# A gated delta rule feeding routed experts: the chunk recurrence as a hand-ordered pipeline of stages

## The chip, the cores and the metric

The kernel runs on one core of a Trainium2 chip. The metric is the device time of one execution in microseconds (us). Before the change the median of three runs is 1243.71 us (1240.04 to 1244.63).

## What is computed

All data is float32: `q`, `k`, `v` of (4, 8, 768, 48) (batch, heads, positions, head size) and `beta` of (4, 8, 768). A delta rule runs over the positions of each head, with a 48x48 state:

```
k_n = k / (norm(k) + 1e-06)
for t in range(S):
    y[t]  = q[t] @ state
    v_old = state.T @ k_n[t]
    state = state + beta[t] * outer(k_n[t], v[t] - v_old)
```

The eight heads of a position are then one row `x` of 384 values (3072 rows). A router takes the best of 8 experts by cosine, with the softmax weight of the best; each expert is `relu(x @ w1[e]) @ w2[e]` with 1024 hidden units, weighted by the router's weight.

## The kernel before, in words

**Attention.** Positions are taken in 12 chunks of 64 (`C`). A tile's 128 partitions hold the 64 positions of one chunk of two batches (g = 0, 1), so that two tiles (p = 0, 1) cover the four batches; the free dimension holds 8 heads by 48. Two chunks make a superchunk (6 of them), and a superchunk's four tiles are numbered j.

`front(s)` (L197) does what needs no state: it loads K, Q, V (`load`, L185), squares and sums the keys (L206, L207), takes the root with GpSimd's pow (L208), scales the keys (L217) and multiplies them by beta (L220), transposes keys and queries on TensorE (L231), multiplies K by K and Q (L239), and masks both products with beta (L245 for A, L246 for P).

`invert(s, A)` (L252) needs the inverse of (1 + A) for each chunk and head. Its four 32x32 diagonal blocks per pair of chunks go through DRAM (`a_dram`, L257, L260), so that 128 partitions hold 128 blocks; VectorE eliminates row by row in 31 steps of two instructions (L267, L269); the inverses go back through DRAM (`t_dram`, L271, L273), are transposed (L275), and TensorE builds the lower 32x32 blocks from them (L285 to L295).

`step(s, j, ...)` (L299) is the recurrence of one tile: the state times keys and queries (L319), the residual R (L321), the solve Z (L329), the new state (L341, added on VectorE in L343), the outputs (L348, L351), then their squares, transposes and router products (L353 to L363). `route(s, ...)` (L365) works out expert, weight and slot of the four tiles, writes the rows to `x_dram` (L395), and scatters the row numbers into `idmap` with four indirect DMAs (L415).

**Order.** Each engine takes its instructions in one fixed order and waits for whatever the head of its queue needs. The tile framework's scheduler orders them by priority around the program's text, which asks for `front` and `invert` of the next superchunk ahead of the four steps of this one:

```
        if s + 1 < NS:
            ahead = front(s + 1)
            Wn = invert(s + 1, ahead[0])
        for j in range(J):
            step(s, j, kts[j], pts[j], kbs[j], vs[j], W, xc, ssx, lz)
        route(s, xc, ssx, lz)
```

**Experts.** Afterwards the rows are processed in 19 tiles of 256 slots: `fetch` (L473) reads the slots of a tile from `idmap`, gathers its rows (L485) and loads its expert's weights (L479, L481); `experts` (L489) transposes (L496), multiplies (L503, L509) and scatters the results (L513). The change does not touch this stage.

Of the kernel before, what the change touches and what calls it, by code (L numbers as in the profile page):

```python
# [15 lines left out]
C = 64  # L16
# [5 lines left out]
def kernel(  # L22
# [28 lines left out]

    nc = tc.nc
# [7 lines left out]
    NS, J = NC // 2, 2 * P2  # L60

    cpool = ctx.enter_context(tc.tile_pool(name="const", bufs=1))
    ps = ctx.enter_context(tc.tile_pool(name="ps", bufs=1, space=bass.MemoryType.PSUM))
    x_dram = tc.dram_tile([N + 1, Dm + 1], F32, name="x_dram")
    idmap = tc.dram_tile([NMAP, 1], I32, name="idmap")
    a_dram = tc.dram_tile([2, 4, J * H, Q, Q], F32, name="a_dram")
    t_dram = tc.dram_tile([2, 4, J * H, Q, Q], F32, name="t_dram")

    def two():
        return ps.tile([128, 2, 512], F32, name="two", tag="two", bufs=3)  # L70

    def one(shape):
        return ps.tile(shape, F32, name="one", tag="one", bufs=2)
# [6 lines left out]
    half = cpool.tile([128, J, H], F32, name="half")  # L80
# [30 lines left out]
    ac = att.enter_context(tc.tile_pool(name="ac", bufs=1))  # L111

    with tc.tile_pool(name="pre", bufs=1) as pre:
        bt = pre.tile([P2 * H, NC, 2, C], F32, name="bt")
        for p in range(P2):
            for g in range(2):
                nc.scalar.dma_start(out=bt[p * H:(p + 1) * H, :, g, :],
                                    in_=beta[2 * p + g].rearrange("h (c t) -> h c t", t=C))
        emb = pre.tile([E, Dm], F32, name="emb")
        nc.scalar.dma_start(out=emb, in_=moe_expert_emb)  # L120
        rtau = ac.tile([128, 1], F32, name="rtau")
        nc.scalar.dma_start(out=rtau, in_=moe_tau.broadcast_to([128, 1]))
        nc.vector.reciprocal(rtau, rtau)

        psB = one([128, NC, P2 * H])
        for c in range(NC):
            nc.tensor.transpose(psB[:, c, :], bt[:, c].rearrange("p g t -> p (g t)"), ident[0:P2 * H, 0:P2 * H])
        betaT = ac.tile([128, NC, P2, H], F32, name="betaT")
        nc.vector.tensor_copy(betaT.rearrange("p c b h -> p c (b h)"), psB)


        esq = pre.tile([E, Dm], F32, name="esq")
        ess = pre.tile([E, 1], F32, name="ess")
        nc.scalar.activation(esq, emb, ACT.Square, accum_out=ess)
        nc.gpsimd.tensor_tensor(out=ess, in0=ess, in1=half[0:E, 0, 0:1], op=ALU.pow)
        nc.vector.tensor_scalar_add(ess, ess, 1e-6)
        nc.vector.reciprocal(ess, ess)
        nc.vector.tensor_scalar_mul(esq, emb, ess)
        psE = one([128, KC, E])
        for j in range(KC):  # L140
            nc.tensor.transpose(psE[:, j, :], esq[:, j * 128:(j + 1) * 128], ident[0:E, 0:E])
        enT = ac.tile([128, KC, E], F32, name="enT")
        nc.vector.tensor_copy(enT, psE)

    io = att.enter_context(tc.tile_pool(name="io", bufs=2))
    wk = att.enter_context(tc.tile_pool(name="wk", bufs=2))
# [4 lines left out]
    nc.vector.tensor_scalar(later[0:C, 0, :], mask_su[0:C, 0:C], 1.0, None, op0=ALU.mult)  # L151
# [8 lines left out]
    eye = ac.tile([128, Q, Q], F32, name="eye")  # L160
    nc.gpsimd.memset(eye, 0.0)
    nc.gpsimd.affine_select(out=eye, in_=eye, compare_op=ALU.not_equal, fill=1.0, base=0,
                            pattern=[[1, Q], [-1, Q]], channel_multiplier=0)


    Qs, KNs, KBs, PIs = [], [], [], []
    for i in range(4):
        Qs.append(ac.tile([128, H, 64], F32, name=f"Qp{i}"))
        nc.gpsimd.memset(Qs[i], 0.0)
    for i in range(4):  # L170
        KNs.append(ac.tile([128, H, 64], F32, name=f"KN{i}"))
# [12 lines left out]

    def load(c):  # L185
        Ks, Vs = [], []
        for p in range(P2):
            Kt = io.tile([128, H, D], F32, name="K", tag="K", bufs=4)
            Vt = io.tile([128, H, D], F32, name="V", tag="V", bufs=8)
            for dst, src in ((Kt, k), (Qs[(c * P2 + p) % len(Qs)][:, :, 0:D], q), (Vt, v)):  # L190
                for g in range(2):
                    nc.sync.dma_start(out=dst[64 * g:64 * g + 64],
                                      in_=src[2 * p + g, :, c * C:(c + 1) * C, :].rearrange("h t d -> t h d"))
            Ks.append(Kt)
            Vs.append(Vt)
        return Ks, Vs


    def front(s):

        data = [load(2 * s + i) for i in range(2)]
        rn = wk.tile([128, J, H], F32, name="rn", tag="rn")
        for j in range(J):
            Ksq = wk.tile([128, H, D], F32, name="Ksq", tag="Ksq")
            Kt = data[j // P2][0][j % P2]
            nc.gpsimd.tensor_tensor(Ksq, Kt, Kt, op=ALU.mult)  # L206
            nc.vector.tensor_reduce(rn[:, j], Ksq, axis=AX.X, op=ALU.add)  # L207
        nc.gpsimd.tensor_tensor(out=rn, in0=rn, in1=half, op=ALU.pow)  # L208
        nc.vector.tensor_scalar_add(rn, rn, 1e-6)
        nc.vector.reciprocal(rn, rn)  # L210
        A = wk.tile([128, J, H, C], F32, name="A", tag="A")
        kts, pts, kbs, vs = [], [], [], []
        for j in range(J):
            c, p = 2 * s + j // P2, j % P2
            n = c * P2 + p
            kn, kb, qp = KNs[n % len(KNs)], KBs[n % len(KBs)], Qs[n % len(Qs)]
            nc.gpsimd.tensor_tensor(kn[:, :, 0:D], data[j // P2][0][p],  # L217
                                    rn[:, j].unsqueeze(2).broadcast_to([128, H, D]), op=ALU.mult)
            bh = betaT[:, c, p]
            nc.gpsimd.tensor_tensor(kb[:, :, 0:D], kn[:, :, 0:D], bh.unsqueeze(2).broadcast_to([128, H, D]),  # L220
                                    op=ALU.mult)
            mb = wk.tile([128, 2, NP, C], F32, name="mb", tag="mb")
            for hh in range(2):
                nc.gpsimd.tensor_tensor(mb[:, hh], later.broadcast_to([128, NP, C]),
                                        bh.rearrange("p (a b) -> p b a", b=2)[:, hh].unsqueeze(2)
                                        .broadcast_to([128, NP, C]), op=ALU.mult)
            KQ = wk.tile([128, NP, 2, 2, C], F32, name="KQ", tag="KQ", bufs=8)
            for i, src in enumerate((kn, qp)):
                psT = one([128, NP, 2, C])
                for hp in range(NP):  # L230
                    nc.tensor.transpose(psT[:, hp].rearrange("p g t -> p (g t)"),  # L231
                                        src[:, 2 * hp:2 * hp + 2, :].rearrange("p h d -> p (h d)"), ident)
                nc.scalar.activation(KQ[:, :, :, i, :], psT, ACT.Copy)
            psG = two()
            for hp in range(NP):
                for g in range(2):
                    for hh in range(2):
                        r = slice(64 * hh, 64 * hh + D)
                        nc.tensor.matmul(psG[64 * g:64 * g + 64, hh, 128 * hp:128 * hp + 128],  # L239
                                         lhsT=KQ[r, hp, g, 0, :], rhs=KQ[r, hp, g, :, :],  # L240
                                         start=True, stop=True, skip_group_check=True)
            pg = psG.rearrange("p a (b i t) -> p (a b) i t", i=2, t=C)
            Pt = wk.tile([128, H, C], F32, name="P", tag="P", bufs=8)
            mbf = mb.rearrange("p a b t -> p (a b) t")
            nc.vector.tensor_tensor(A[:, j], pg[:, :, 0, :], mbf, op=ALU.mult)  # L245
# [307 lines left out]
```

## Time and profile before

| | us |
|---|---|
| median of the runs | 1243.71 |
| the profiled execution | 1250.58 |
| its span, first to last instruction | 1248.6 |
| TensorE busy in the span | 781.4 |
| VectorE busy | 304.9 |
| ScalarE busy | 160.7 |
| GpSimd busy | 240.6 |

The profiled execution lies 0.55% above the median, and 2 us of it lie outside the span. PE is TensorE's matmuls, PEld its weight loads, DVE is VectorE, ACT ScalarE, POOL GpSimd, SP the sync engine that issues most DMAs. The clock is the share of TensorE's full clock that was granted: 1.00 is 2.4 GHz, 0.50 is 1.2 GHz.

### The profile page before, as it was taken

To read this page: it belongs to the slowest core of one execution; us is meant where nothing else is said; L and a number is where in the kernel's file an instruction comes from. 1 tells how busy PE (TensorE), PEld (TensorE's weight loads), DVE (VectorE), ACT (ScalarE), POOL (GpSimd) and SP (SyncE) were. 2 spreads that over 40 slices of the span, in tenths; PEclk is the share of its full clock that TensorE was granted. 3 is DMA by queue.
4 is the path that set the end of the run, shared out by engine and by line. 5 is a ranking of instruction groups with operands and counts; after the bars stand their busy time and mean duration, and the time that the engine had idled before them with its cause. 6 is when DMAs were issued, how large, how long until landed. Compare 5 with 4: busy or idle time off the path is not lost. (4 is left out here: it accounts for less than half of the span.)

```text
span 1248.6 us, 18748 instructions
## 1 busy us (share of the span) xinstructions
PE 781.4 (63%) x8033; PEld 632.4 (51%) x8033; DVE 304.9 (24%) x821; ACT 160.7 (13%) x313; POOL 240.6 (19%) x259
## 2 busy tenths in 40 slices
PE   0306128801980088209813985299999999999996
PEld 0206028601870077208703885276766766767764
DVE  3471440344033502360243022001001001011010
ACT  0102012200220022002201221010100100101100
POOL 5553400231013201300110011111111111111110
PEclk9755555655555555655565555599999999999998
DMA  4522310331025101410111010654554455455520
GB/s 83 110 42 44 72 34 8 56 68 34 8 48 83 34 8 35 71 34 9 39 34 35 2 27 26 215 179 154 175 187 156 159 180 179 138 175 181 167 70 0
DMA packets 167668, 104.93 MB, mean 84 GB/s; under 512 B 133089, under 2 KB 155801, under 8 KB 167586
## 3 DMA queue, kind: packets, MB, share of 16 engines
q1 hardware_dynamic: 161232, 91.28, 27.2%
q0 software_dynamic: 5632, 12.24, 3.5%
q8 instruction: 63, 1.03, 0.4%
q10 hardware_dynamic: 722, 0.23, 0.1%
q14 instruction: 19, 0.16, 0.1%
HBM read 87.84 MB, written 18.63 MB: 85 GB/s over the span
## 5 line engine op out<-in xcount | busy, mean ns | idle before, releaser
L285 PE MATMUL one<-Tz,A 64*64 64x32 f32 x768 | 45.7, 291 | 313.5 <-ACT Tz L277 313.5
L503 PE MATMUL two<-xTm,w 128*128 128x256 f32 x912 | 203.4, 383 | 12.3 <-DVE xTm L497 12.3
L285 PEld LDWEIGHTS one<-Tz,A 64*64 64x64 f32 x768 | 43.7, 222 | 314.6 <-ACT Tz L277 314.6
L509 PE MATMUL one<-w,hT 128*128 128x384 f32 x608 | 199.2, 486 | 0.0
L503 PEld LDWEIGHTS two<-xTm,w 128*128 128x128 f32 x912 | 172.8, 191 | 40.0 <-DVE xTm L497 17.0
L509 PEld LDWEIGHTS one<-w,hT 128*128 128x128 f32 x608 | 115.5, 190 | 76.5
L512 DVE TENSOR_SCALAR y<-one,xg 128x384 f32<-128x384 f32 x38 | 23.5, 618 | 389.5 <-PE one L509 389.5
L505 ACT ACTIVATE hT<-two 128x512 f32<-128x512 f32 x76 | 45.4, 597 | 412.6 <-PE two L503 412.6
L513 POOL DMA_INDIRECT out_dram<-y,ids x38 | 38.1, 1004 | 242.4 <-DVE y L512 242.4
L267 DVE TENSOR_TENSOR tmp<-Bk,Tk 128x31 f32<-128x31 f32 (+15 forms) x186 | 71.1, 382 | 52.5 <-DMA Bk<-a_dram 46.6
L269 DVE TENSOR_TENSOR Tk<-Tk,tmp 128x31 f32<-128x31 f32 (+15 forms) x186 | 68.2, 367 | 5.9
L485 POOL DMA_INDIRECT xg<-x_dram,ids x38 | 37.3, 982 | 133.1 <-DMA ids<-idmap 84.7
L319 PE MATMUL two<-S,KQ 48*64 48x48 f32 x1408 | 56.8, 294 | 6.5 <-DVE P L246 6.5
L220 POOL TENSOR_TENSOR KB<-KN,betaT 128x384 f32<-128x384 f32 x24 | 20.5, 859 | 206.0 <-PE two L341 206.0
L293 PE MATMUL one<-Wd,PI 64*64 64x32 f32 x768 | 46.1, 292 | 14.6 <-ACT PI L288 14.6
L319 PEld LDWEIGHTS two<-S,KQ 48*64 48x64 f32 x1408 | 47.6, 202 | 13.2 <-issue 12.2
L343 DVE TENSOR_TENSOR S<-S,two 128x384 f32<-128x384 f32 x22 | 12.2, 554 | 168.7 <-PE two L341 168.7
L293 PEld LDWEIGHTS one<-Wd,PI 64*64 64x64 f32 x768 | 42.8, 220 | 17.8 <-ACT PI L288 17.8
L329 PE MATMUL one<-R,W 64*64 64x48 f32 x768 | 49.2, 303 | 0.0
L277 ACT ACTIVATE Tz<-Td,first 128x1024 f32<-128x1024 f32 x6 | 6.9, 1148 | 324.8 <-DMA Td<-t_dram 324.8
L329 PEld LDWEIGHTS one<-R,W 64*64 64x64 f32 x768 | 47.0, 223 | 0.1
L348 PE MATMUL two<-Z,P 64*64 64x48 f32 x768 | 46.3, 303 | 0.7 <-ACT Z L332 0.6
(129 smaller groups left out, 758.2 us busy)
## 6 DMA issues: line engine op xcount, KB each, us to landing
w<-in_moe_w_dram SPq DMA_DIRECT2D x38, 1536.0 KB, 6.7
x_dram<-xc SPq DMA_DIRECT2D x24, 192.5 KB, 3.1
Qp<-in_q_dram SPq DMA_DIRECT2D x48, 96.0 KB, 4.2
K<-in_k_dram SPq DMA_DIRECT2D x48, 96.0 KB, 2.7
V<-in_v_dram SPq DMA_DIRECT2D x48, 96.0 KB, 2.7
a_dram<-A SPq DMA_DIRECT2D x24, 128.0 KB, 2.8
Bk<-a_dram SPq DMA_DIRECT2D x6, 512.0 KB, 3.7
t_dram<-Tk SPq DMA_DIRECT2D x6, 512.0 KB, 2.6
```

Of the source, the lines that this page charges most:

```text
L267: nc.vector.tensor_tensor(tv, Bk[:, i, i + 1:Q].unsqueeze(2).broadcast_to(sh), Tk[:, i:i + 1, 0:i + 1].broadcast_to(sh), op=ALU.mult)
L269: nc.vector.tensor_tensor(Tk[:, i + 1:Q, 0:i + 1], Tk[:, i + 1:Q, 0:i + 1], tv, op=ALU.subtract)
L285: nc.tensor.matmul(psP[r, h, :], lhsT=A[r, j, h, :], rhs=Tz[r, j * H + h, :], start=True, stop=True, skip_group_check=True)
L293: nc.tensor.matmul(psW[r, h, :], lhsT=PI[r, h, :], rhs=Wd[r, j * H + h, :], start=True, stop=True, skip_group_check=True)
L319: nc.tensor.matmul(pv[64 * g:64 * g + 64, hh, hp, :], lhsT=KQ[r, hp, g, i, :], rhs=Sp[r, g, hp, :], start=(hp == 0), stop=True, skip_group ...
L329: nc.tensor.matmul(psZ[r, h, :], lhsT=W[r, j * H + h, :], rhs=Rf[r, h, :], start=True, stop=True, skip_group_check=True)
L348: nc.tensor.matmul(yv[r, hh, hp, :], lhsT=Pt[r, hh * NP + hp, :], rhs=Z[r, hh * NP + hp, :], start=(c == 0 and hp == 0), stop=True, skip_g ...
L485: nc.gpsimd.indirect_dma_start(out=x, out_offset=None, in_=x_dram[:, :], in_offset=bass.IndirectOffsetOnAxis(ap=ids[:, t:t + 1], axis=0))
L503: nc.tensor.matmul(psH[:, 0, i * T:(i + 1) * T], lhsT=w1[:, j, (f + i) * 128:(f + i + 1) * 128], rhs=xT[:, j, :], start=(j == 0), stop=(j ...
L505: nc.scalar.activation(hT[:, f:f + 2, :], psH[:, 0].rearrange("p (i t) -> p i t", i=2), ACT.Relu)
L509: nc.tensor.matmul(psO, lhsT=hT[:, f, t * 128:(t + 1) * 128], rhs=w2[:, f, :], start=(f == 0), stop=(f == NF - 1))
L513: nc.gpsimd.indirect_dma_start(out=out[:, :], out_offset=bass.IndirectOffsetOnAxis(ap=ids[:, t:t + 1], axis=0), in_=y, in_offset=None, bou ...
```

## The change

The attention part is written anew, as stages per chunk c, inside a region in which each engine takes its instructions in the order of the text. One iteration of the loop issues the norms of chunk c+6, the transposes and products of c+5, part of an elimination, the lower blocks of c+1, and the recurrence of c; it runs from c = -6 to 11. The elimination is a generator, of which `steps(n)` issues n steps. Routing takes four chunks at once (8 tiles) and is a generator too, worked off by `fill(n)`; it ends with eight indirect DMAs. Beta leaves keys and masks: `weigh` multiplies the blocks by it and starts the inverse from it. The state of two heads is block-diagonal, so that one product of 128 rows by 96 columns takes the place of two of 48 by 48. The sum of the states stays in PSUM, and ScalarE copies it to SBUF (`keep`). Keys are loaded twice (`Kf` and `Kl`), and Q in halves.

```diff
+    def squares(c):
...
+            nc.gpsimd.tensor_tensor(Ksq, Kf[c][p], Kf[c][p], op=ALU.mult)
...
+            nc.vector.tensor_reduce(rns[c][:, p], sq[p], axis=AX.X, op=ALU.add)
...
+    def root(c):
+        nc.gpsimd.tensor_tensor(out=rns[c].rearrange("p a h -> p (a h)"), in0=rns[c].rearrange("p a h -> p (a h)"),
+                                in1=half, op=ALU.pow)
...
+    def blocks_in(s):
+        Bks[s] = wk.tile([128, Q, Q], F32, name="Bk", tag="Bk")
+        nc.sync.dma_start(out=Bks[s], in_=a_dram[s % 2].rearrange("b i n s t -> (b i n) s t"))
+
+    def weigh(s):
+        Tks[s] = wk.tile([128, Q, Q], F32, name="Tk", tag="Tk")
+        nc.gpsimd.memset(Tks[s], 0.0)
+        nc.gpsimd.tensor_copy(Tks[s].rearrange("p a b -> p (a b)")[:, 0:Q * Q:Q + 1], bb[:, s])
+        nc.gpsimd.tensor_tensor(Bks[s], Bks[s], bb[:, s].unsqueeze(1).broadcast_to([128, Q, Q]), op=ALU.mult)
...
+    def by_state(ps1, c, p, i):
+
+        for hp in range(NP):
+            for g in range(2):
+                nc.tensor.matmul(ps1[64 * g:64 * g + 64, 2 * D * hp:2 * D * (hp + 1)], lhsT=KQs[c, p][:, hp, g, i, :],
+                                 rhs=state(c, p)[:, g, hp].rearrange("p a d -> p (a d)"),
+                                 start=(hp == 0), stop=True, skip_group_check=True)
...
+    def keep(c, p):
+        for hh in range(2):
+            r = slice(64 * hh, 64 * hh + D)
+            nc.scalar.activation(state(c + 1, p)[r, :, :, hh, :], sv[r, :, p], ACT.Copy)
...
+        yield
         for j in range(J):
             nc.gpsimd.indirect_dma_start(
                 out=idmap[:, :], out_offset=bass.IndirectOffsetOnAxis(ap=slot_i[:, j:j + 1], axis=0),
...
+    for c in range(-6, NC):
+        cf, cn, cl = c + 5, c + 6, c + 1
+        odd = c % 2 == 1
+        if odd and 0 <= (c + 1) // 2 < NS:
+            inverses_back((c + 1) // 2)
+        if odd:
+            elim = eliminate((c + 3) // 2) if 0 <= (c + 3) // 2 < NS else None
+        if has(cn):
+            squares(cn)
+        if has(cl):
+            if c < 0:
+                Kl[cl], Vl[cl] = load(k, cl, "Kl", 2), load(v, cl, "V", 4)
+            unit_keys_again(cl, 0)
+        if has(cn):
+            root(cn)
+        if has(cl):
+            unit_keys_again(cl, 1)
+        if has(c):
+            Rs = [residual(c, p) for p in both]
+        if has(cf):
+            transposes(cf, 0, 0)
+            transposes(cf, 0, 1)
+            transposes(cf, 1, 0)
+        steps(3)
+        if has(c):
+            solve(c, 0, Rs[0])
+        if has(cf):
+            transposes(cf, 1, 1)
+        if has(c):
+            solve(c, 1, Rs[1])
+        if has(cf):
+            products(cf, 0)
+        steps(3)
+        if has(cn):
+            inverse_norms(cn)
+            unit_keys(cn)
+            load_q(cn) if cn > 0 else None
+        if has(cn + 2):
+            Kf[cn + 2] = load(k, cn + 2, "K", 4)
+        if has(c + 2) and c + 1 >= 0:
+            Kl[c + 2], Vl[c + 2] = load(k, c + 2, "Kl", 2), load(v, c + 2, "V", 4)
+        if has(c) and c < NC - 1:
+            for p in both:
+                update(c, p)
+        if has(cf):
+            products(cf, 1)
+            blocks_out(cf)
+            if cf % 2 == 1:
+                blocks_in(cf // 2)
+                weigh(cf // 2)
+        if has(c) and c < NC - 1:
+            for p in both:
+                keep(c, p)
+        steps(3)
+        if odd and 0 <= (c + 1) // 2 < NS:
+            turn((c + 1) // 2)
+        fill(6)
+        if has(c):
+            outputs(c, 0)
+            steps(3)
+            fill(6)
+            outputs(c, 1)
+        steps(20 if not odd else 4)
+        if has(cl):
+            lower1(cl)
+        if has(c):
+            store(c)
+            xTs = [turned(c, p) for p in both]
+        if has(cl):
+            lower2(cl)
+        if has(c):
+            for p in both:
+                squared(c, p)
+            logits(c, xTs)
+            fill(20)
+            if c % RC == RC - 1:
+                behind.append(route(c // RC))
+    fill(1000)
```

## Rows read from the trace of the kernel before

**Rows 1.** Busy time by stretch: length, busy us of each engine, clock, DMA share, GB/s.

```profile
306.00:434.00 128.00, 61.46 (x1096) 55.70 (x1096) 42.06 (x115) 18.90 (x39) 26.32 (x27) 0.54 0.21 38
...
802.00:1249.00 447.00, 416.33 (x1634) 301.63 (x1632) 43.00 (x76) 45.38 (x76) 73.52 (x74) 0.98 0.47 155
```

**Rows 2.** The same view, inside the period of 306 to 434 us.

```profile
306.00:325.00 19.00, 14.96 (x264) 14.43 (x266) 1.25 (x1) 5.54 (x10) 0.00 (x0) 0.50 0.01 2
325.00:362.00 37.00, 33.50 (x608) 30.58 (x606) 4.73 (x12) 8.56 (x21) 4.35 (x5) 0.50 0.09 18
362.00:380.00 18.00, 12.88 (x229) 10.69 (x229) 9.14 (x31) 4.79 (x9) 5.74 (x7) 0.78 0.49 90
380.00:434.00 54.00, 0.11 (x8) 0.00 (x0) 26.94 (x71) 0.00 (x0) 16.23 (x15) 0.50 0.28 48
```

**Rows 3.** Who waited for whom: total us, times, longest.

```profile
PE one L285 <- ACT Tz L277: 313.5, 6, 58.4
```

**Rows 4.** The timeline of that period's inverse: start us, us, engine, line.

```profile
385.97 2.24 SPq L257 DMA_DIRECT2D a_dram<-A  x4
397.83 0.19 DVE L267 TENSOR_TENSOR tmp<-Bk,Tk 128x31 f32<-128x31 f32 x1 [10.84 <-DMA Bk<-a_dram]
...
430.08 0.19 DVE L269 TENSOR_TENSOR Tk<-Tk,tmp 128x31 f32<-128x31 f32 x1
437.31 1.15 ACT L277 ACTIVATE Tz<-Td,first 128x1024 f32<-128x1024 f32 x1 [61.44 <-DMA Td<-t_dram]
```

**Rows 5.** Groups of instructions: busy us, mean ns, idle before.

```profile
L267 DVE TENSOR_TENSOR tmp<-Bk,Tk 128x31 f32<-128x31 f32 (+15 forms) x186 | 71.1, 382 | 52.5 <-DMA Bk<-a_dram 46.6
L269 DVE TENSOR_TENSOR Tk<-Tk,tmp 128x31 f32<-128x31 f32 (+15 forms) x186 | 68.2, 367 | 5.9
L343 DVE TENSOR_TENSOR S<-S,two 128x384 f32<-128x384 f32 x22 | 12.2, 554 | 168.7 <-PE two L341 168.7
L206 POOL TENSOR_TENSOR Ksq<-K 128x384 f32<-128x384 f32 x24 | 20.5, 855 | 60.5 <-DMA K<-in_k_dram 44.6 <-DVE rn L207 15.7
L208 POOL TENSOR_TENSOR rn<-rn,half 128x32 f32<-128x32 f32 x6 | 33.0, 5504 | 23.4 <-DVE rn L207 23.4
```

**Rows 6.** Timeline, the first superchunk's inverse comes back.

```profile
99.57 1.15 ACT L277 ACTIVATE Tz<-Td,first 128x1024 f32<-128x1024 f32 x1 [54.30 <-DMA Td<-t_dram]
```

**Rows 7.** Timeline: an elimination step beside GpSimd, and the same form alone.

```profile
72.44 1.96 POOL L220 TENSOR_TENSOR KB<-KN,betaT 128x384 f32<-128x384 f32 x2
72.78 0.93 DVE L267 TENSOR_TENSOR tmp<-Bk,Tk 128x252 f32<-128x252 f32 x1
...
80.51 0.42 DVE L267 TENSOR_TENSOR tmp<-Bk,Tk 128x252 f32<-128x252 f32 x1
```

**Rows 8.** Timeline: eight K loads in a row on the SP queue.

```profile
394.19 5.36 SPq L192 DMA_DIRECT2D K<-in_k_dram  x8
```

**Rows 9.** Stretches around the rise of the clock, columns as in rows 1.

```profile
117.80:120.60 2.80, 2.80 (x15) 2.28 (x12) 0.00 (x0) 1.58 (x3) 0.83 (x1) 0.50 0.00 0
120.60:129.00 8.40, 7.18 (x150) 5.58 (x148) 4.42 (x7) 3.37 (x6) 6.41 (x10) 1.00 0.54 100
```

**Rows 10.** Timeline: TensorE at either clock, transposes (L231) and products (L239).

```profile
117.84 1.11 PE L231 MATMUL one<-ident,KN 128*128 128x128 f32 x4
...
367.92 1.99 PE L239 MATMUL two<-KQ 48*64 48x128 f32 x32
371.17 1.10 PE L239 MATMUL two<-KQ 48*64 48x128 f32 x32 [0.25 <-ACT KQ L233]
```

**Rows 11.** Timeline, from the last attention output to the first expert tile.

```profile
764.89 0.50 ACT L351 ACTIVATE xc<-two 128x384 f32<-128x384 f32 x1 [2.04 <-PE two L348]
774.52 1.03 POOL L415 DMA_INDIRECT idmap<-tokid,slot_i  x1 [7.35 <-DVE ends L455]
...
791.72 0.38 SPq L477 DMA_DIRECT2D ids<-idmap  x1
801.64 1.51 PE L496 MATMUL one<-ident,xg 128*128 128x128 f32 x6 [30.25 <-DMA xg<-x_dram,ids]
```

More of the change, by code (lines that the diff above doesn't have):

```diff
@@ L79 @@
     nc.vector.memset(ones, 1.0)
-    half = cpool.tile([128, J, H], F32, name="half")
+    half = cpool.tile([128, P2 * H], F32, name="half")
     nc.vector.memset(half, 0.5)
@@ L111, with bank @@
     ac = att.enter_context(tc.tile_pool(name="ac", bufs=1))
-    with tc.tile_pool(name="pre", bufs=1) as pre:
-        bt = pre.tile([P2 * H, NC, 2, C], F32, name="bt")
+    wk = att.enter_context(tc.tile_pool(name="wk", bufs=2))
+    ps = att.enter_context(tc.tile_pool(name="ps", bufs=1, space=bass.MemoryType.PSUM))
+    def bank(tag, bufs):
+        return ps.tile([128, 512], F32, name=tag, tag=tag, bufs=bufs)
+    Qs, KNs = [], []
+    for i in range(P2):
+        Qs.append(ac.tile([128, NP, 2, 64], F32, name=f"Qp{i}"))
+        nc.gpsimd.memset(Qs[i], 0.0)
+        KNs.append(ac.tile([128, NP, 2, 64], F32, name=f"KN{i}"))
+        nc.gpsimd.memset(KNs[i], 0.0)
@@ L115, with heads, load, load_q @@
+    def heads(t):
+        return t.rearrange("p (a b) d -> p b a d", a=2)
+    def load(src, c, name, bufs):
+        ts = []
+        for p in range(P2):
+            t = wk.tile([128, H, D], F32, name=name, tag=name, bufs=bufs)
+            for g in range(2):
+                nc.sync.dma_start(out=t[64 * g:64 * g + 64],
+                                  in_=src[2 * p + g, :, c * C:(c + 1) * C, :].rearrange("h t d -> t h d"))
+            ts.append(t)
+        return ts
+    def load_q(c):
         for p in range(P2):
@@ L126 @@
[L126 to L146, printed above, removed]
+                for hh in range(2):
+                    nc.sync.dma_start(out=Qs[p][64 * g:64 * g + 64, :, hh, 0:D],
+                                      in_=q[2 * p + g, hh * NP:(hh + 1) * NP, c * C:(c + 1) * C, :]
+                                      .rearrange("h t d -> t h d"))
@@ new lines @@
+    manual = ctx.enter_context(ExitStack())
+    manual.enter_context(tc.manual_schedule())
+    Kf = {0: load(k, 0, "K", 4)}
+    load_q(0)
+    Kf[1] = load(k, 1, "K", 4)
+    Kl, Vl = {}, {}
+    bb = ac.tile([128, NS, Q], F32, name="bb")
+    for b in range(4):
+        for i in range(2):
+            for p in range(P2):
+                o = (2 * b + i) * BL + p * H
+                nc.scalar.dma_start(out=bb[o:o + H], in_=beta[2 * p + b // 2].rearrange(
+                    "h (s i a r) -> i a h s r", i=2, a=2, r=Q)[i, b % 2])
@@ L199, in front @@
[L199 to L203, printed above, removed]
-            Ksq = wk.tile([128, H, D], F32, name="Ksq", tag="Ksq")
[L205 to L245, printed above, removed]
-            nc.vector.tensor_tensor(Pt, pg[:, :, 1, :], mbf, op=ALU.mult)
-            kts.append(KQ)
-            pts.append(Pt)
-            kbs.append(kb)
-            vs.append(data[j // P2][1][p])
-        return A, kts, pts, kbs, vs
@@ L296, in invert @@
[L296 to L325 removed]
+            nc.sync.dma_start(out=Td[Q * b:Q * b + Q], in_=t_dram[s % 2, b].rearrange("n s c -> s n c"))
@@ new lines, in outputs, with store @@
+        if p == 0:
+            xcs[c] = wk.tile([128, P2, Dm], F32, name="xc", tag="xc", bufs=3)
+        nc.scalar.activation(xcs[c][:, p].rearrange("p (a b d) -> p b a d", a=2, d=D),
+                             psY[:, 0:Dm].rearrange("p (b a d) -> p b a d", a=2, d=D), ACT.Copy)
+    def store(c):
+        for g in range(2):
+            nc.sync.dma_start(x_dram[0:N, 0:Dm].rearrange("(p g s) d -> g s p d", g=2, s=S)
+                              [g, c * C:(c + 1) * C], xcs[c][64 * g:64 * g + 64])
@@ L434, with fill, has, steps @@
-    att.close()
+                in_=tokid[:, b * RC + j // P2, j % P2:j % P2 + 1], in_offset=None)
+    behind = []
+    def fill(n):
+        while n and behind:
+            if next(behind[0], 0) == 0:
+                behind.pop(0)
+            else:
+                n -= 1
+    def has(c):
+        return 0 <= c < NC
+    both = range(P2)
+    elim = None
+    def steps(n):
+        for _ in range(n):
+            if elim is not None:
+                next(elim, None)
+    for c in range(-6, NC):
[75 more added lines that the diff above has]
+                behind.append(route(c // RC))
@@ L437, with two, one @@
+    fill(1000)
+    manual.close()
+    att.close()
+    ps = ctx.enter_context(tc.tile_pool(name="psm", bufs=1, space=bass.MemoryType.PSUM))
+    def two():
+        return ps.tile([128, 2, 512], F32, name="two", tag="two", bufs=3)
+    def one(shape):
+        return ps.tile(shape, F32, name="one", tag="one", bufs=2)
     wt = ctx.enter_context(tc.tile_pool(name="wt", bufs=2))
```

379 lines of the change are left out of this document (203 added, 176 removed).

## The prediction

> **What bounds the kernel now.** The busy time by stretch comes first, since attention and experts have different limits. The experts run from 802 us to the end, 447 us with TensorE busy 416.33 us at clock 0.98 [rows 1]: TensorE bounds them, and the change leaves them alone. In attention a period for two chunks takes 128 us, and no engine is busy for half of it: TensorE 61.46 us, VectorE 42.06, GpSimd 26.32, ScalarE 18.90 [rows 1]. Inside the period [rows 2] the reader sees engines that take turns: TensorE has the lower blocks and the four steps (306 to 362 us, clock 0.50) and most of the front; then for 54 us it does nothing while VectorE eliminates. The list of waits names it: TensorE stood 313.5 us in six waits for Tz [rows 3], which needs the inverses back from DRAM. The timeline [rows 4] shows that chain: blocks leave at 385.97 us, the first step runs at 397.83, the last at 430.08, and the inverses are back at 437.31; 51 us in all. So attention is bound by a serial chain, 64 us per chunk, and the change is about overlap.
>
> **The change part by part.** The sum is made against the profiled execution: 1248.6 us of span, 2 us around it, together 0.55% above the median of the runs.
>
> *VectorE.* Its 42.06 us per period are 21.0 per chunk [rows 1]. The sum of states moves to PSUM, two additions of 554 ns per chunk [rows 5]; masks, residuals, key sums and 31 steps per two chunks stay. The steps are 71.1 + 68.2 us in six eliminations [rows 5], 11.6 us per chunk. That leaves 20 us per chunk, which already holds some collisions with GpSimd: a step of 0.42 us takes 0.93 beside a GpSimd multiplication of 0.98 [rows 7]. In the new order nearly every GpSimd operation falls beside elimination steps; some seven per chunk at half a microsecond each add at most 3.5. I take 22 to 23 us.
>
> *GpSimd.* Squares, unit keys and second keys are six multiplications of about 0.855 us [rows 5]; the root of 16 columns is half of 5504 ns [rows 5], 2.75; `weigh` every second chunk is some 3.3 us, its product of 1024 columns scaled from the 384 of the 855 ns. About 9.5 us per chunk, hidden. What the root costs an elimination step that runs beside it, no row shows: VectorE always waits for it. Bounds are nothing, if only multiplications collide, and 2.75 us per chunk. I take 1 us, since VectorE can take key sums and masks there, and keep both ends.
> By the Trainium skill ("SBUF — State Buffer", Terms) VectorE and GpSimd arbitrate for a shared port pair that is held for a whole instruction, and the loser fully blocks; the 0.93 us agrees, and by that rule the upper bound would hold, 1.75 us more per VectorE-bound iteration.
>
> *TensorE.* 61.46 us per period are 30.7 per chunk, mostly at clock 0.50 [rows 1]. The block-diagonal state halves the count of state products but they stream 96 columns in place of 48, at best 2 us less; the lower blocks and the rest stay. At 0.50 throughout it is about 32 to 33 us, because a third of the front ran at 1.00 (a set of products takes 1.99 us at 0.50 and 1.10 at 1.00 [rows 10]); at 1.00 about 17. So the clock decides whether TensorE or VectorE bounds an iteration.
>
> *ScalarE* has 18.90 us per period [rows 1], 9.5 per chunk; the four state copies add 2 us, hidden.
>
> *The SP queue and the round trip.* An iteration issues 20 loads (8 of them halves of Q), four block stores and two row stores. K loads take 5.36 us for eight, 0.67 each [rows 8]. The halves wait for the transposes, so `blocks_out` comes about 14 us into an iteration. In every second (even) one `weigh` waits for the blocks to come back, 11.9 us from store to first use [rows 4], plus 2.3 us of product and 0.9 of the next squares, which stand behind `weigh` on GpSimd and ahead of everything on VectorE. So an even iteration takes at least 29 us whatever the clock.
>
> *Prologue.* The first inverse came back at 99.57 us [rows 6]. Six iterations run ahead of the first recurrence, and that chain is in them, with `weigh` (2.3 us) and the sums, masks and norms of three further chunks, 4.3 us each, between its steps. Estimate: 115 us.
>
> *Routing.* The four indirect DMAs at the end wait for each other: 774.52 to 791.72 us, 4.3 each [rows 11]. Now there are eight in a row. After chunk 7's batch GpSimd has little else to do (8 us lost). After chunk 3's batch they stand at the end of iteration 4, ahead of the squares of chunk 11, behind which VectorE stands at the head of iteration 5: 8 x 4.3 = 34 us in which nothing can go on. At the end, eight in place of four add 17 us, and the longer batch 4.5: the stretch from the last output (ended 765.39) to the first expert tile (801.64 [rows 11]) grows from 36 us to 58.
>
> *The sum*, with the clock at 1.00 for part of each iteration (TensorE some 25 us): prologue 115; iterations 0, 2, 4, 6 at 29.5 and 1, 3, 5 at 27: 199; the stall of iteration 5: 34; iterations 7 and 8, without a front, at 23: 46; 9 and 10 at 21, with 8 lost: 50; 11 to its last output: 12; the tail 58; the experts 447. Together 961 us of span, 288 less than now; from the median, 956 us.
>
> **The rivals.**
> *The clock stays at 0.50.* For it: the four steps kept TensorE busy 33.50 of 37 us without the clock rising [rows 2]. Against: it rose from 0.50 to 1.00 at 120.6 us after 2.8 us of little but transposes [rows 9, 10], and each new iteration has 12 of them behind products of 128 rows. Then TensorE bounds: prologue 117, seven iterations at 33.5, less 2 in the first (232), 34, twice 25.5, twice 25.5, 4, 13.5, 58, 447: 1008 us of span, 1003 against the median.
> The Trainium skill speaks for this rival ("TensorE: Matmul & The Clock Gate", Part 4): transposes do not count as busy work there and do not bring the full clock; the stretch of rows 9 does not bear that out.
> *The clock stays at 1.00.* Then the round trip bounds even iterations (29) and VectorE the odd ones (23): 115, 185, 34, twice 18, twice 14 with 14 lost, 8, 58, 447: 925, or 920 against the median. For it: once up, it stayed at 1.00 to the end of that front [rows 9]. Against: TensorE would wait a third of each iteration.
> *The fixed order does not overlap (slower).* Each queue head could wait for another engine in turn: TensorE for the masks and turned inverses, VectorE for products and logits. Place: the middle of an iteration. Price: TensorE 33, VectorE 20 and ScalarE 9.5 in series, 62.5 us for seven iterations, 50 and 37 for the later ones: 437 + 100 + 111; with 115 + 34 + 8 + 58 + 447 that is 1310 us of span. All outside the iterations is 662 us, so it decides from (1248.6 - 662) / 12 = 49 us per iteration. Against it: three PSUM banks for each of two kinds of product let TensorE run ahead, and 22 us of elimination need nothing from it.
> *The pipeline does not do what it says*: it overlaps, but a round trip slowed by the loads (its DMAs share the 16 engines with 20 loads) adds 10 to 30 us to every even iteration, two of them in the prologue: 1020 to 1150 us.
>
> **How the numbers follow.** Part-time full clock 0.42 (956), clock at 0.50 0.27 (1003), at 1.00 0.20 (920), slow round trip 0.06, serial order 0.04, something faster than all, as when iteration 5 loses nothing (920 - 34 = 886), 0.01. The range reaches from 895, below the fast case with most of its stall kept, to 1045, the 0.50 case with the root's upper bound and a slower round trip (some 40 us more); it leaves out about 0.1. Half a per cent, 6 us, is about what a measurement of this kernel can tell from no change. Faster 0.95, same 0.01, slower 0.04.
>
> **What would show it.** Right: in the waits, Tz's 313.5 us are gone; iterations of 23 to 34 us; one gap of over 30 us on TensorE and VectorE about iteration 5 with GpSimd in idmap DMAs; eight of those ahead of the experts; the expert stretch unchanged at 447 us. The clock between the prologue and the tail tells the first three cases apart. Wrong: iterations over 40 us, a prologue beyond 140 us, an expert stretch of another length, or GpSimd's indirect DMAs no longer waiting for each other.

## The result, and the profile after

The kernel after the change takes **975.61 us** (median of four runs, 973.78 to 983.60) beside 1242.81 us for the one before on the same chip: a ratio of 0.7861, 95% interval 0.7820 to 0.7901. The forecast was 956 us with a range of 895 to 1045, so time and sign were right and the forecast was 2.0% short. Of run 8, one execution at 921.55 us, 2% above the fastest of its kernel, is left out. The profiled execution is the longest of the four, 983.60 us with a span of 980.7; the forecast sum of 961 us of span is set against that.

The head of the profile of the kernel after:

```profile
span 980.7 us, 17338 instructions
PE 718.4 (73%) x7305; PEld 577.7 (59%) x7305; DVE 277.0 (28%) x727; ACT 167.0 (17%) x330; POOL 226.7 (23%) x228
```

TensorE's work fell only from 781.4 to 718.4 us, VectorE's from 304.9 to 277.0. So at most 63 of the 268 us that the span lost can be less work on TensorE; the rest was waiting. The sum can be checked stretch by stretch: the busy time by stretch, cut at the logits copies and key sums that end the iterations. The first row is iteration 0; the prologue took the 120.20 us ahead of it.

```profile
core 0: us, PE busy (x) PEld busy (x) DVE busy (x) ACT busy (x) POOL busy (x), PEclk, DMA share, GB/s
120.20:154.23 34.03, 21.77 (x483) 19.98 (x480) 16.94 (x47) 12.36 (x25) 9.79 (x9) 0.80 0.51 113
154.23:180.24 26.01, 22.29 (x440) 20.82 (x442) 18.95 (x45) 8.28 (x18) 9.43 (x9) 0.63 0.61 100
180.24:213.72 33.48, 23.54 (x526) 21.33 (x524) 16.16 (x43) 11.61 (x24) 9.63 (x9) 0.86 0.46 106
213.72:239.72 26.00, 21.46 (x440) 20.12 (x442) 19.00 (x44) 8.28 (x18) 9.43 (x9) 0.70 0.59 94
239.72:288.57 48.85, 29.90 (x516) 27.67 (x516) 21.81 (x75) 10.44 (x22) 10.41 (x8) 0.64 0.39 80
288.57:323.02 34.45, 2.60 (x18) 2.13 (x14) 0.17 (x1) 1.68 (x3) 8.80 (x10) 0.55 0.05 6
323.02:348.94 25.92, 21.36 (x440) 19.99 (x442) 18.27 (x43) 8.28 (x18) 9.79 (x10) 0.70 0.42 82
348.94:369.55 20.61, 20.27 (x484) 18.50 (x486) 13.69 (x37) 9.84 (x21) 0.00 (x0) 0.91 0.30 70
369.55:388.06 18.51, 18.18 (x404) 17.11 (x406) 14.95 (x37) 7.89 (x19) 6.52 (x6) 0.78 0.75 154
388.06:419.39 31.33, 26.72 (x438) 25.14 (x438) 17.12 (x67) 8.16 (x18) 1.02 (x1) 0.61 0.33 61
419.39:436.84 17.45, 16.11 (x376) 15.04 (x374) 2.31 (x5) 7.68 (x17) 4.79 (x5) 0.79 0.02 3
436.84:468.45 31.61, 22.26 (x404) 20.76 (x406) 1.28 (x3) 7.83 (x17) 6.31 (x8) 0.61 0.26 52
468.45:477.57 9.12, 9.06 (x195) 8.19 (x195) 1.28 (x3) 1.97 (x5) 0.00 (x0) 0.84 0.01 2
477.57:532.41 54.84, 3.06 (x20) 2.68 (x20) 9.67 (x55) 2.33 (x7) 11.42 (x11) 0.54 0.20 62
532.41:980.70 448.29, 417.67 (x1634) 302.35 (x1634) 43.00 (x76) 45.41 (x76) 73.52 (x74) 0.98 0.47 155
```

In iterations 0 to 3 a chunk takes 26 to 34 us where it took 64, and in a row of 26 us TensorE is busy for 21 to 22: the engines overlap. The 54 us without TensorE [rows 2] and the wait for Tz [rows 3] have no successor of that size. What takes their place shows in the timeline (start and duration in us, engine, line, operation; in brackets the idle time before and what ended it). The chain of an even iteration: iteration 0, SP's queue, then GpSimd, then VectorE.

```profile
134.18 3.13 SPq L126 DMA_DIRECT2D K<-in_k_dram  x4
137.35 2.67 SPq L126 DMA_DIRECT2D Kl<-in_k_dram  x4
140.07 3.21 SPq L126 DMA_DIRECT2D V<-in_v_dram  x4
143.38 2.20 SPq L271 DMA_DIRECT2D a_dram<-AP  x4
147.19 0.34 SPq L276 DMA_DIRECT2D Bk<-a_dram  x1
...
151.07 2.34 POOL L282 TENSOR_TENSOR Bk<-Bk,bb 128x1024 f32<-128x1024 f32 x1 [14.87 <-DMA Bk<-a_dram]
153.37 1.61 POOL L214 TENSOR_TENSOR Ksq<-K 128x384 f32<-128x384 f32 x2
...
154.23 0.55 DVE L217 TENSOR_REDUCE rn<-Ksq 128x8 f32<-128x384 f32 x1 [10.88 <-POOL Ksq L214]
```

Nine microseconds of loads stand ahead of the blocks on SP; GpSimd waits 14.87 us for the blocks with the next squares behind it, and VectorE 10.88 us for those. In iteration 4 routing's root stands there too, and all engines follow it (GpSimd, VectorE, TensorE, then the idmap DMAs, first and last of eight):

```profile
264.14 2.34 POOL L282 TENSOR_TENSOR Bk<-Bk,bb 128x1024 f32<-128x1024 f32 x1 [8.81 <-DMA Bk<-a_dram]
266.44 1.64 POOL L429 TENSOR_TENSOR ssx<-ssx,half 128x8 f32<-128x8 f32 x1
...
268.12 0.17 DVE L431 TENSOR_SCALAR ssx<-ssx 128x8 f32<-128x8 f32 x1 [11.80 <-POOL ssx L429]
...
270.52 0.66 PE L455 MATMUL f<-oh,mask_su 128*128 128x64 f32 x2 [18.61 <-DVE oh L450]
...
289.05 1.22 POOL L482 DMA_INDIRECT idmap<-tokid,slot_i  x1 [20.97 <-DVE slot_i L479]
...
321.17 0.96 POOL L482 DMA_INDIRECT idmap<-tokid,slot_i  x1 [2.83 <-DMA idmap<-tokid,slot_i]
322.16 1.61 POOL L214 TENSOR_TENSOR Ksq<-K 128x384 f32<-128x384 f32 x2
```

### The profile page after: what moved, and what is told of

It reads as the page before. It is cut to its first block, busy times and chain, and to the rows that moved or that the text cites. A ratio compares the mean times of both kernels' runs of the same rounds, so it can differ in the third digit from the quotient of the medians.

```text
span 980.7 us, 17338 instructions
## 1 busy us (share of the span) xinstructions
PE 718.4 (73%) x7305; PEld 577.7 (59%) x7305; DVE 277.0 (28%) x727; ACT 167.0 (17%) x330; POOL 226.7 (23%) x228
## 5 line engine op out<-in xcount | busy, mean ns | idle before, releaser
L357 PE MATMUL r<-R,W 64*64 64x48 f32 x704 | 30.5, 251 | 59.8 <-DVE R L348 59.8
L357 PEld LDWEIGHTS r<-R,W 64*64 64x64 f32 x704 | 28.2, 167 | 63.7 <-DVE R L348 59.9
L259 PE MATMUL f<-KQ 48*64 48x128 f32 x768 | 39.0, 336 | 31.2 <-DVE AP L263 31.2
L482 POOL DMA_INDIRECT idmap<-tokid,slot_i x24 | 23.5, 981 | 129.9 <-DMA idmap<-tokid,slot_i 69.6
L259 PEld LDWEIGHTS f<-KQ 48*64 48x64 f32 x768 | 31.5, 170 | 35.0 <-DVE AP L263 32.8
L337 PE MATMUL r<-S,KQ 128*64 128x96 f32 x704 | 50.6, 312 | 0.0
L326 PE MATMUL f<-Wd,PI 64*64 64x32 f32 x768 | 38.4, 272 | 16.2 <-ACT PI L318 16.1
L326 PEld LDWEIGHTS f<-Wd,PI 64*64 64x64 f32 x768 | 36.9, 198 | 19.3 <-ACT PI L318 18.3
L337 PEld LDWEIGHTS r<-S,KQ 128*64 128x64 f32 x704 | 43.0, 181 | 2.4 <-issue 1.0
L247 ACT ACTIVATE KQ<-f 128x512 f32<-128x512 f32 x48 | 27.8, 597 | 88.9 <-PE f L246 88.5
```

The costliest lines, as they stand in the source:

```text
L259: nc.tensor.matmul(psG[hh][64 * g:64 * g + 64, 128 * hp:128 * hp + 128], lhsT=KQ[r, hp, g, 0, :], rhs=KQ[r, hp, g, :, :], start=True, stop ...
L326: nc.tensor.matmul(psW[r, m, :], lhsT=PI[r, m, :], rhs=Wds[s][r, n + m, :], start=True, stop=True, skip_group_check=True)
L337: nc.tensor.matmul(ps1[64 * g:64 * g + 64, 2 * D * hp:2 * D * (hp + 1)], lhsT=KQs[c, p][:, hp, g, i, :], rhs=state(c, p)[:, g, hp].rearran ...
L357: nc.tensor.matmul(psZ[r, h, :], lhsT=Ws[c][r, p * H + h, :], rhs=R[r, h, :], start=True, stop=True, skip_group_check=True)
```

## The experiments

Each ran beside the kernel before on its chip. A kernel with the ratio 0.7861 would have taken 981.5 us in the first four, 980.9 in the next four and 978 in the last four; differences are against that, and its interval makes about 5 us of each uncertain.

**1. Routing's root earlier.**

```diff
             load_q(cn) if cn > 0 else None
+        if has(c) and c % RC == 0:
+            fill(1)
```

> Only the first operation of routing is moved: GpSimd's root of the row sums of a batch is issued in the middle of the first iteration after the batch (c = 4, 8), behind the unit keys, and no longer at its end, behind the weighing of the blocks. Theory A: iteration 4 takes 48.9 us, where iterations 0 and 2 take 34.0 and 33.5, since this root stands behind the weighing in GpSimd's queue, which waits 8.8 us for the blocks, and VectorE and TensorE then wait for routing (11.8 and 18.7 us). Then iteration 4 falls to 34 to 37 us and the kernel to 961 to 964 us. Theory B: iteration 4 is long because of the routing work itself, some 6 us on VectorE and the products with ohf in TensorE's queue: then it stays above 44 us and the kernel within 0.5% of 975.6 us. The gap of 34 us behind it stays with both.

965.96 us (965.73 to 968.13), ratio 0.7743 (0.7725 to 0.7760): 15.5 us less. Iteration 4 and the gap, by stretch:

```profile
237.71:272.65 34.94, 25.62 (x514) 23.53 (x514) 24.20 (x75) 10.21 (x22) 10.55 (x8) 0.74 0.48 103
272.65:308.16 35.51, 2.56 (x20) 2.09 (x16) 0.17 (x1) 1.61 (x3) 8.77 (x10) 0.55 0.11 13
```

Iteration 4 now takes 34.94 us, near iteration 2's 33.4; the gap stays. Theory A: one operation of 1.64 us at the wrong place in GpSimd's queue cost 14.

**2. The idmap DMAs spread.** `route` puts them on a list, and an iteration issues three:

```diff
+        pending.extend((slot_i, b, j) for j in range(J))
...
             unit_keys_again(cl, 1)
+        scatter(1)
```

> The eight indirect DMAs of a batch into idmap are no longer issued in a row: three are issued per iteration, in iterations 5 to 7 and 9 to 11; those of the last batch stay at the end. Theory A: they wait for each other and GpSimd for them, so that the gap of 34.3 us at the head of iteration 5 is all theirs, and those of the second batch hold up iteration 10 by some 8 us: the gap goes, iteration 5 stays near 26 us, and the kernel takes 931 to 942 us. Theory B: behind that gap stands another wait (the elimination and its round trip, or the K loads), so that only some 20 us come back: 950 to 958 us. Theory C: each DMA holds GpSimd 4 us wherever it stands, so that VectorE loses the same time in pieces: 970 us or more.

939.14 us (934.84 to 941.12), ratio 0.7517 (0.7490 to 0.7544): 42 less. The gap is gone: iteration 5 begins 0.1 us behind iteration 4 and takes 22.9 us, and iteration 10 takes 17.2 in place of 31.6.

```profile
290.77:313.63 22.86, 21.73 (x456) 19.80 (x455) 19.01 (x44) 10.19 (x21) 10.34 (x9) 0.80 0.51 83
407.18:424.39 17.21, 16.67 (x404) 15.40 (x406) 1.28 (x3) 7.43 (x16) 3.12 (x4) 0.90 0.13 26
```

Theory A, the second batch included; the spread DMAs still wait for each other, up to 5.4 us, but now beside other engines' work. The second batch cost 14.4 us in iteration 10, not the 8 of theory and forecast.

**3. Loads behind the blocks.** The three lines with `load(k, cn + 2, ...)` and `load(k, c + 2, ...)`, `load(v, ...)` move below `weigh(cf // 2)`.

> On the sync engine's queue the loads of K, of K again and of V stand behind the stores of the blocks and their way back, no longer ahead of them; the loads of Q stay. Theory A: these loads make the store of the blocks some 9 us late (in iteration 0 they are issued from 134.2 to 143.3 us, while the masks were done at about 134), and the weighing and everything behind it with it: iterations 0, 2 and 4 fall by 8 to 9 us each, from 34 to 25 or 26, and the prologue by up to 10: 940 to 952 us. Theory B: TensorE, at a clock between 0.50 and 1.00, bounds these iterations a few us below their 34 us: 962 to 970 us. Theory C: the later loads of K and V become the wait: 975 us or more.

963.02 us (957.18 to 965.91), ratio 0.7702 (0.7668 to 0.7737): 18 less, between A and B. Iterations 0 and 2 fall to 26.5 and 25.0 us, as A has it; but the prologue and iteration 4 fall by 3 us only, and iteration 7 grows from 18.5 to 26.5. SP's queue and VectorE around it:

```profile
341.79 3.03 SPq L126 DMA_DIRECT2D Kl<-in_k_dram  x4
344.87 2.67 SPq L126 DMA_DIRECT2D V<-in_v_dram  x4
...
349.85 0.55 SPq L297 DMA_DIRECT2D t_dram<-Tk  x1
355.22 2.19 SPq L299 DMA_DIRECT2D Td<-t_dram  x4
...
360.83 1.25 DVE L304 STREAM_TRANSPOSE Wd<-Td 128x1024 f32<-128x1024 f32 x1 [6.19 <-DMA Td<-t_dram]
```

The loads now stand ahead of the store of the inverses, which go through DRAM on the same queue: stored at 349.85, 5.1 us after the logits (in the kernel after 1.3 us ahead of them, 368.21 to 369.55), they let VectorE wait 6.19 us. What the blocks gained, the inverses lost in part.

**4. Weighing later.**

```diff
-                weigh(cf // 2)
+                start_inverse(cf // 2)
...
             unit_keys_again(cl, 1)
+        if odd and 0 <= (c + 3) // 2 < NS:
+            weigh((c + 3) // 2)
```

> The product that weighs the blocks with beta is issued in the next iteration, behind the squares, the root and the unit keys, and no longer at the end of the even one, ahead of them. Theory A: what makes even iterations 33.5 to 34 us long is that GpSimd waits for the blocks (14.9, 14.4 and 8.8 us) with the squares behind it, and VectorE for the squares (10.9 and 12.7 us): iterations 0 and 2 fall to 25 to 27 us, iteration 4 by as much or more, since routing's root no longer stands behind the wait: 940 to 955 us. Theory B: the wait moves on to VectorE, where the first elimination steps stand ahead of the masks: a part of it, 3 to 4 us per even iteration, is all that comes back: 960 to 968 us.

958.75 us (954.01 to 964.95), ratio 0.7696 (0.7661 to 0.7732): 23 less, 21 by the ratios. Both theories hold a part. Iterations 0, 2 and 4 take 24.7, 21.8 and 29.6 us (A; in iteration 4 routing's root no longer stands behind the wait, so that the gain of run 1 is in this one), but iteration 3 takes 31.0 and the prologue 125.7, since VectorE waits with the first elimination step (iteration 3, timeline):

```profile
212.79 0.19 DVE L292 TENSOR_TENSOR tmp<-Bk,Tk 128x31 f32<-128x31 f32 x1 [11.35 <-POOL Bk L284]
```

**5. The sum of states back on VectorE.**

```diff
-            nc.scalar.activation(state(c + 1, p)[r, :, :, hh, :], sv[r, :, p], ACT.Copy)
+            nc.vector.tensor_tensor(state(c + 1, p)[r, :, :, hh, :], state(c, p)[r, :, :, hh, :],
+                                    sv[r, :, p], op=ALU.add)
```

> One part is undone: PSUM holds only the update of one chunk, and VectorE adds it to the state before, four additions of 64 partitions by 192 per chunk (some 0.35 to 0.55 us each), in place of ScalarE's four copies. Theory A, the prediction's: VectorE has 17 to 19 us of work in iterations of 26 to 34, so that the sum in PSUM is worth nothing by itself: 973 to 980 us. Theory B: the additions stand in VectorE's queue behind masks and elimination steps, and the next products by the state wait for them: 1.5 to 2.2 us per chunk, 992 to 1000 us.

990.26 us (979.76 to 991.17), ratio 0.7939 (0.7926 to 0.7952): 9 us more, between the two. The profiled execution is the one at 979.76, so that the profile doesn't show where the others lost it; in it the 44 additions take 550 ns each, 24.2 us that nearly all lie beside other work. So the PSUM sum, with its copies on ScalarE, is worth about 9 us, up to 1%; where it earns that stays open.

**6. The scheduler's order.** The two lines of `manual_schedule` are taken out.

> The region of fixed order is taken away, all else is kept: the framework's scheduler orders the same instructions. Theory A: the gain comes from the order written out by hand, for the scheduler puts each chunk's chain together, so that elimination and recurrence wait for each other as before: over 1100 us. Theory B: the gain comes from the text, which issues the front five chunks ahead and has no chain through one iteration; the scheduler keeps to that: 930 to 1020 us, and the stall of eight idmap DMAs may even go, since it may put squares ahead of them.

994.72 us (989.27 to 1000.10), ratio 0.7957 (0.7928 to 0.7987): 14 us more, theory B. The new stages bring 253 of the 267 us in the scheduler's order too; which part of them (the front five chunks ahead, no chain through one iteration, fewer products) brings how much, no run separates. The 14 us are a balance. Waits in run 6, then VectorE's wait for squares in run 6 and in the kernel after (total us, times, longest):

```profile
PE f L324 <- DVE Wd L302: 104.5, 5, 33.5
...
DVE rn L215 <- POOL Ksq L212: 5.3, 2, 2.6
...
DVE rn L217 <- POOL Ksq L214: 86.1, 14, 34.3
```

The scheduler lets TensorE wait 104.5 us for the turned inverses (Wd), which the order by hand avoids, but it spares VectorE most of the 86.1 us behind the blocks and the idmap DMAs, which the order by hand brought.

**7. Spread and late weighing together**, weighing early in the prologue, first elimination steps behind the masks.

> Together: the idmap DMAs spread over iterations (as in the run before), routing's root in mid-iteration, and the weighing behind the squares, the latter only once the recurrence runs (in the prologue it cost 5 us); the first three elimination steps of an odd iteration go behind the first masks, so that the masks don't wait for the weighing. If the gains add: of 981 us on that chip, 41 us for the idmap DMAs, 21 for the weighing, 5 for the prologue, 3 to 5 for the steps: 905 to 915 us. If TensorE at clock 0.50 bounds the iterations as soon as the waits are gone, half of the last three is lost: 918 to 928 us.

913.41 us (911.87 to 918.50), ratio 0.7328 (0.7301 to 0.7355): 67.5 us less of the 70 to 72 that the expectation adds up, so the gains add. The 14 us of run 1 are no term of their own beside those of run 4.

**8. Routing of two chunks** (`RC = 2` in the kernel of 7).

> The same with routing every two chunks: one size is changed. At the end four idmap DMAs instead of eight stand between the last chunk and the experts, some 4.1 us each (490.13 to 518.57 us for seven steps), but routing's 6 us on VectorE comes three times more. If the end alone counts: 15 to 18 us less than the run before, some 892 us. If routing's waits (its root on GpSimd, ohf in TensorE's queue) come into every even iteration, 3 x 5 us are given back: within 0.5% of it.

909.57 us (903.49 to 913.81), ratio 0.7282 (0.7233 to 0.7331): no difference that shows. TensorE's wait ahead of the experts falls from 49.8 to 30.5 us, but iterations with routing give it back; iteration 2 by stretch:

```profile
171.81:208.66 36.85, 27.61 (x492) 25.37 (x492) 21.31 (x68) 10.52 (x22) 10.05 (x10) 0.69 0.54 113
```

The same iteration in the kernel of 7, which has no routing in it:

```profile
171.93:192.89 20.96, 20.62 (x503) 18.85 (x502) 16.99 (x42) 9.95 (x21) 8.26 (x8) 0.94 0.58 111
```

**9. More products for the clock.** Four transposes of the identity behind `lower1` and behind `lower2`.

> The kernel after the change, with four more transposes of the identity behind each half of the lower blocks, into a bank that nobody reads: 8 per chunk, 0.15 us each at clock 1.00 (0.88 us for six) and 0.26 at 0.50, so 1.2 to 2.1 us more work on TensorE per chunk. In iterations 6 to 8 TensorE hardly waits; the granted clock falls from 1.00 to 0.50 while it runs the second half of the lower blocks and the logits (about 369 and 383 us) and is back only behind the next products by the state: the two halves of the lower blocks, the transposes between them and the logits take 6.7 us at 1.00 (362.99 to 369.44) and 11.5 at 0.50. Theory A: the clock is lost to what runs there, and stays up with the transposes between: 3 us less in each of the iterations 5 to 11, 950 to 962 us of the 976. Theory B: it falls all the same, and the transposes cost their time where TensorE bounds: 983 to 995 us. Theory C: nothing to see, within 0.5%: TensorE's work is not what sets the length.

982.90 us (977.03 to 987.69), ratio 0.7884 (0.7860 to 0.7908): 5 more, which its interval doesn't tell from none, so theory A falls as a gain. Its mechanism isn't shown either. In the kernel after, by stretch, the clock fell between 366 and 372 us, with TensorE busy throughout:

```profile
366.00:372.00 6.00, 6.00 (x108) 5.91 (x106) 2.64 (x11) 2.25 (x7) 1.99 (x1) 0.75 0.71 239
```

In run 9, at the same work with the transposes between, it did not, but neither did it in run 10, which has no such transposes; and in iteration 8 of run 9 it stayed at 0.50 through eight of them (two rows of run 9, one of run 10):

```profile
364.00:370.00 6.00, 6.00 (x148) 5.72 (x144) 4.45 (x16) 3.44 (x7) 0.00 (x0) 1.00 0.48 96
405.00:432.00 27.00, 25.56 (x372) 24.16 (x374) 9.92 (x44) 6.46 (x15) 2.05 (x2) 0.50 0.27 55
...
350.00:356.00 6.00, 6.00 (x128) 5.60 (x124) 3.78 (x14) 3.16 (x8) 1.06 (x1) 1.00 0.68 187
```

In runs 1, 2 and 3, without the transposes too, the logits of iteration 6 also ran at 1.00; in run 5 the clock fell there as in the kernel after. So neither these products nor the transposes decide it alone, and what does stays open.

**10. Embeddings ahead of beta** on ScalarE's queue: the 16 loads of `bb` move behind `esq`.

> The kernel after the change, with the router's temperature and embeddings loaded ahead of the 16 loads of beta on ScalarE's queue. Those take 12.30 us to issue, and GpSimd stood 12.17 us for the embedding's norm, with the first squares of keys behind it at 20.30 us. Theory A: the prologue is one chain from these squares, 120 us in place of the forecast 115 since it begins late: 8 to 12 us less, 964 to 968 us. Theory B: the K loads and the round trips set the prologue (the sync engine needs until 31 us for its first loads, and GpSimd waits for the blocks until 59.95): under 4 us less, 972 us or more.

965.79 us (963.98 to 969.63), ratio 0.7755 (0.7743 to 0.7767): 12 less. The first squares begin at 8.38 us in place of 20.30, iteration 0 at 107.7 in place of 120.2: theory A, the prologue is one chain. In the kernel after, ScalarE's queue and GpSimd:

```profile
0.81 12.30 ACTq L152 DMA_DIRECT2D bb<-in_beta_dram  x16
...
16.72 0.58 POOL L165 TENSOR_TENSOR ess<-ess,half 8x1 f32<-8x1 f32 x1 [12.17 <-ACT esq L164]
...
20.30 1.70 POOL L214 TENSOR_TENSOR Ksq<-K 128x384 f32<-128x384 f32 x2
```

**11. Routing in two iterations**, in the kernel of 8: by smaller arguments of `fill`, VectorE's part comes in the even iteration, the products with `mask_su` and `ones` in the odd one.

> The version with routing of two chunks, spread idmap DMAs and late weighing, in which routing is divided over two iterations: VectorE's part up to the choice of expert in the even one, the products with mask_su and ones and what follows in the odd one. Before, iterations 2 and 6 took 36.9 and 35.1 us there, against 21.0 and 24.3 in the version that routes four chunks, which have no routing in them. Theory A: that time goes as TensorE's queue no longer waits for the choice: 10 to 25 us less than 911 us, 885 to 900. Theory B: the time is VectorE's and GpSimd's own for three more batches, wherever it stands: 905 to 915 us.

898.55 us (897.75 to 901.57), ratio 0.7221 (0.7211 to 0.7231): the time is theory A's, but only some 8 us less than run 8 by the ratios. Iteration 2 takes 30.0 us in place of 36.9, still more than the 21.0 without routing, so that a part of theory B holds.

**12. The gains together**: 11 with the embeddings first.

> The version before (routing of two chunks in two iterations, spread idmap DMAs, late weighing) with the embeddings ahead of beta on ScalarE's queue. Theory A: the prologue's 11 us add to it, since nothing else in the prologue moved: 886 to 890 us of the 898.6. Theory B: with less to wait for, the first iterations lose part of it again to the round trip or the clock: 892 to 899 us.

888.09 us (885.92 to 892.42), ratio 0.7141 (0.7121 to 0.7161): theory A. It beats both kernels, 9% under the one after the change.

## Why the prediction was right, and where not

**Bound and sign held.** The kernel was bound by a serial chain, and the change overlaps it. Of the rivals the serial order is out by far (its bound was 49 us per iteration; only iteration 4 came there). The gain doesn't hang on the order by hand: the new stages overlap in the scheduler's order too (run 6). That the time came within 2% is in part luck: the terms below miss by up to 19 us, and some misses cancel. The 956 us also leave out the 2 us outside the span; 961 and 2, less 0.55%, make 958.

**The clock**, on which three cases hung, came out as forecast, part-time: 0.61 to 0.91 in the iterations. About 352 us, for one, it rose to 1.00 behind the products by the state. Most falls come where TensorE waits (143 to 150 us, 204 to 210, 252 to 258); at 369 us, in the logits behind the second half of the lower blocks, and at 382 and 461 us it fell with TensorE busy. On the rule cited for the rival at 0.50 ("TensorE: Matmul & The Clock Gate", Part 4, of the Trainium skill: transposes do not bring the full clock) run 9 decides nothing, for the clock stayed up without the added transposes too; what speaks against it is still the rise of [rows 9] alone.

**The sum, term by term** (forecast, measured in us):

| | forecast | measured |
|---|---|---|
| prologue | 115 | 120.2 |
| iterations 0 to 3 | 113 | 119.5 |
| iteration 4 | 29.5 | 48.9 |
| stall of iteration 5 | 34 | 34.4 |
| iterations 5, 6 | 56.5 | 46.5 |
| 7 and 8 | 46 | 49.8 |
| 9 and 10 | 50 | 49.1 |
| 11 | 12 | 9.1 |
| tail | 58 | 54.8 |
| experts | 447 | 448.3 |

*The stall* was right in size, place and cause, and run 2 shows it: eight DMAs, some 4.6 us apart. *Tail* and *experts* were right.

*Even iterations* were mis-sized: "`blocks_out` comes about 14 us into an iteration". It came 23 us in (143.38 in an iteration from 120.20). The forecast counted 20 loads but let only those of Q stand ahead of the blocks; K, Kl and V do too, 9.2 us, and run 3 shows what they cost. A second miss took half of it back: from store to first use the blocks needed 7.7 us (143.38 to 151.07), not 11.9. With 23.2 + 7.7 + 2.3 + 0.9 an even iteration takes 34 us, and iterations 0 and 2 took 34.0 and 33.5. So the rival of a round trip slowed by the loads had the right place and the wrong mechanism: the loads delay its start, not the trip. Iteration 6 took 20.6, not 29.5: it has no squares left to stand behind `weigh`, so the round trip that bounded it was no longer on the path.

*Iteration 4* is the step that failed: routing was costed by its DMAs alone. Its root of 1.64 us was never followed along GpSimd's queue, where it stands behind `weigh`; the prediction followed the squares there, but not this. Run 1 prices it at 14 us. An iteration over 40 us was one of the prediction's own signs of being wrong. Iteration 8 (31.3 us) has routing too, but no weighing; run 1 left it at 31.6, so that there it is another cause, which no run took alone. The trace shows TensorE 4.28 us in wait for routing's choice `oh` (L455, 401.16), and then at clock 0.50 from 402 to 417 us.

*Pairs that hide misses*: iteration 7 was 4.5 us shorter than its 23 and iteration 8 8.3 longer; iteration 9 3.5 shorter than its 21, while the idmap DMAs cost iteration 10 14.4 us (run 2), not 8.

*The prologue* came 5 us late, and the prediction doesn't name the 16 loads of beta; run 10 gets 12 back. There it ends at 107.7, so that the rest of the estimate was 7 us too long, and the two misses cancel in part.

*The root beside the elimination*, bounded 0 to 2.75 us and taken as 1, is at the lower bound. The timeline of the kernel after, GpSimd and VectorE, beside a root, beside unit keys, and the last form alone:

```profile
155.73 2.90 POOL L220 TENSOR_TENSOR rn<-rn,half 128x16 f32<-128x16 f32 x1
156.41 0.18 DVE L290 TENSOR_TENSOR tmp<-Bk,Tk 128x31 f32<-128x31 f32 x1
...
133.31 1.65 POOL L229 TENSOR_TENSOR KN<-K,rn 128x384 f32<-128x384 f32 x2 [8.22 <-DVE rn L225]
134.19 1.02 DVE L290 TENSOR_TENSOR tmp<-Bk,Tk 128x240 f32<-128x240 f32 x1
...
249.39 0.40 DVE L290 TENSOR_TENSOR tmp<-Bk,Tk 128x240 f32<-128x240 f32 x1
```

Beside the root a step takes its 0.18 us, beside the multiplication 1.02 in place of 0.40. The size of the step isn't the reason: one of 31 columns took 0.80 us beside a multiplication (run 3, 347.59). VectorE was busy 18.3 to 19.0 us in iterations 1, 3 and 5, not 22 to 23; the root accounts for 1 us of that at most, and the rest isn't taken apart. By the rule of "SBUF — State Buffer", Terms, in the Trainium skill, the steps would have stood until the root ended; there the trace disagrees, and for the multiplication it agrees.

*The state in PSUM* was taken as two additions less on VectorE, worth little; run 5 puts it at 9 us, up to 1%.

## What to carry to other kernels

In a fixed order, walk each queue, those of SP and GpSimd first, and ask of every instruction what stands behind a waiting one: here a root of 1.64 us behind a DRAM round trip cost 14 us, a weighing ahead of the squares 21 to 23 (with that root), and nine microseconds of loads ahead of the blocks 18. DMAs that wait for each other should be issued one at a time between other work, and a load moved out of one round trip's way should be checked against the next. The new stages overlapped in either order, and the order by hand gained only 14 us on balance, since it removed some waits and brought others; finding those in the trace was worth a further 9% (run 12).

## What the runs showed of the hardware

- GpSimd's power operation does not slow VectorE beside it, while a multiplication of 0.8 us does (rows above). Its time goes with the columns: 1.64 us for 8, 2.90 for 16, 5504 ns for 32 [rows 5].
- A DMA costs its queue about the same for half the bytes: eight halves of Q (48 KB each) took 5.24 us to issue where nothing held them up, four loads of K (96 KB each) 2.65. The change halved Q's loads and so doubled their time on SP.
- TensorE's clock fell from 1.00 to 0.50 while the engine waited for nothing, in the stretch from 366 to 372 us shown with run 9; at the same products it stayed at 1.00 in runs 1, 2, 3 and 10. So these products alone do not decide the clock.
